# Windowed attention and two gated layers on one core: what the planner books for the attention's last steps

## The chip, the core and the metric

The kernel runs on one core of a Trainium2 chip. A core has five engines that run their own instruction streams in order: TensorE (PE; its weight loads are shown apart as PEld), VectorE (DVE), ScalarE (ACT), GpSimd (POOL) and SyncE (SP), which issues the DMA transfers here. The metric is the device time of one execution in microseconds (us); lower is better.

## What is computed

The reference, cut to what matters. Shapes: q, k, v are (4, 8, 576, 64); the token matrix between the parts is 2304 x 512.

```python
def _attn_ref(q, k, v):                      # causal, a window of 64 keys
    scores = scale * np.matmul(q, k.transpose(0, 1, 3, 2))
    mask = (rel >= 0) & (rel < 64)
    scores = np.where(mask, scores, -1e9)
    attn = np.exp(scores - np.max(scores, axis=-1, keepdims=True))
    attn = attn / (np.sum(attn, axis=-1, keepdims=True) + 1e-09)
    return np.matmul(attn, v)

x = attn_out.transpose(0, 2, 1, 3).reshape(2304, 512)
g = x @ w_gate                               # 512 x 1536
x = (g / (1 + np.exp(-g))) * (x @ w_val) @ w_out
h = (x @ w1) * (x @ w2) @ w3                 # 1024 wide
return h @ w_out2                            # 2304 x 512
```

The weights and the result keep fp32 accuracy; each fp32 operand is split into a high part and a remainder, and a product takes three passes (high x high, high x remainder, remainder x high).

## The kernel before

**Attention.** It runs in 24 steps, m = 0 to 23. In step m, PE computes the scores `S`, DVE takes their maximum (L420), ACT the exponential (L427), DVE the reciprocal of the sum (L433, L434), POOL multiplies it in (`pexp`, L437), PE transposes the result (`PT`, L446), DVE copies the transpose to SBUF (`ptt`, L452), PE multiplies by v (`PV`, L466), and ACT copies that into the token tiles `X` (L480, L483). The stages are staggered: `PT` of step m is made two steps later and `PV` three steps later, so after the loop an end is left over: one `PV`, and two times `PT`, `ptt`, `PV`. After the loop ACT also loads another function table (L563).

**Operands.** The first gated layer takes its tokens in three groups of 768 (tp = 0, 1, 2). A group is cut in four blocks by seven-product (Strassen-like) algebra; for each product p (in the order 1, 2, 5, 6, 7, 4, 3) and each half m of the 512 channels there is a tile `xo_pm`, made of up to three jobs: a difference of X blocks, in place (L208, DVE), a cast to the high part (L200, ACT), and the remainder (L204, DVE). In the names below the group is left out; the number at a name's end tells tiles of different groups apart. Differences for product 6 overwrite what product 5 reads, so they follow the remainder of 5.

**The gated layer.** `gated` yields one product at a time: six matmuls of 128x384 (L596) into a PSUM bank (`ala`, `gaa`, `bea` for the gate weights, `alb`, `gab`, `beb` for the value weights), then a copy by ACT (L603), additions by DVE (L607), SiLU by ACT (L617) and the gating product by DVE (L614). Units run in the order (gate, value) for group 0, 1, 2, with the products of two units interleaved; then come the next 256 columns of the weights, which first have to be narrowed from 64-bit words and split (L188, L190, L192, L194, L200, L204, L208).

**The planner.** The order of instructions on each engine is fixed when the program is built. Jobs (operand and weight preparation) lie in a queue with costs per engine. The code of the attention and of the products is written out at once, and the planner keeps a clock `plan.now`: `plan.charge` books written work on an engine, `plan.advance(us, but)` lets time pass and then emits every queued job that its books let start before the clock, on engines not in `but`. A job that is emitted early stands ahead of the attention's or the product's own instructions on its engine. `plan.slots` counts free SBUF tiles in the same way, and `hold` gives back those that the attention no longer needs. None of these numbers runs on the chip; they only set the order. Near the attention's end four functions use them: `during_attention` at the end of a step, `filling` inside a step, `drain(0..4)` after the loop (three of its calls take a product from the generator `gate`), and `operands(tp)`, which queues a group's operand jobs.

Of the kernel before, what the change touches and what calls it, by code (L numbers as in the profile page):

```python
# [32 lines left out]
def window_attention_moe_kernel(ctx: ExitStack, tc: tile.TileContext, q, k, v, w_gate, w_val, w_out, w1, w2, w3, w_out2, out):  # L33
# [121 lines left out]
    plan = Plan()  # L155
# [173 lines left out]
    def x_tile(tp, c):  # L329
        if (tp, c) not in X:  # L330
            X[tp, c] = slot([P, TP], F32, f"X{tp}_{c}")
        return X[tp, c]

    def attention(events, filling, drain):
        if True:
            ident, identr = own.tile([P, P], F32, name="ident"), own.tile([P, P], F32R, name="identr")
# [179 lines left out]
            for m in range(NM):  # L516
# [24 lines left out]
                if m == NM - 1:  # L541

                    evac_PT(m - 2)
                else:

                    filling(m)
# [7 lines left out]
                if m == NM - 1:  # L554
                    filling(m)
# [6 lines left out]
            evac_PV(NM - 3)  # L562
            nc.scalar.activation(out=masks[:, 0, :1], in_=masks[:, 1, :1], func=AF.Silu)  # L563
            drain(0)
            for x in range(2):
                emit_PT(NM - 2 + x)
                evac_PT(NM - 2 + x)
                drain(1 + 2 * x)
                emit_PV(NM - 2 + x)
                evac_PV(NM - 2 + x)  # L570
                drain(2 + 2 * x)
# [509 lines left out]
    def loads(n):  # L1081
        while at[0] < min(n, len(coming)):
            coming[at[0]].load()
            at[0] += 1

    def make_to(x, rank=None):

        while at[1] <= coming.index(x):
            plan.rank = rank if rank is not None else 1 if isinstance(coming[at[1]], Weights) else 2
            loads(at[1] + 1)  # L1090
            coming[at[1]].make()
            at[1] += 1
            loads(at[1] + 2)
            plan.rank = 0
# [72 lines left out]
    gate = gated(xop1, left1, order1, AF.Silu, h1d, events1)  # L1167


    HELD = {18: 24, 19: 22, 20: 18, 21: 16, 22: 12, 23: 7}  # L1170
# [3 lines left out]
    def hold(n):  # L1174
        plan.slots += held[0] - n
        held[0] = n

    def operands(tp):
        xop1[tp] = Operands([X[tp, c] for c in range(KC)], f"xo{tp}")

    def during_attention(m):
        if m in HELD:
            hold(HELD[m])
        if m in (1, 3):
            loads(1 + m // 2)
        if m == 3:
            make_to(left1[0, 1], 0)
        if m in (13, 20):
            operands(m // 20)
        plan.fill(("DVE",) if m not in HELD or m < 23 else ("DVE", "ACT"))  # L1190

    def filling(m):
        for e, cost in (("DVE", 2.75), ("ACT", 3.2), ("POOL", 2.6)):
            plan.charge(e, cost)
        if m == 23:
            plan.advance(3.1, ("DVE", "ACT", "POOL", "SP"))
        else:
            plan.advance(3.85, ("ACT", "POOL", "SP"))

    def drain(n):  # L1200
        hold(HELD_END[n])
        for e, cost in (("DVE", (0.4, 1.1, 0.0, 1.1, 0.0)), ("ACT", (3.0, 0.0, 0.6, 0.0, 0.6))):
            plan.charge(e, cost[n])
        if n == 4:
            operands(2)
        else:
            next(gate) if n in (0, 1, 3) else plan.advance(0.8)

    with tc.manual_schedule():
        plan.shut.add("POOL")  # L1210
        attention(during_attention, filling, drain)
        plan.ahead = 1.0
        for _ in gate:
            pass
        for _ in project(rows, wos, events_p):
            pass
        on(events2, len(order2) - 6, lambda: make_to(w3s[-1]))
        begin_e, run_e = final(rows2)

        def put_all():  # L1220
            for j in by:
                plan.need(j)
            begin_e()
        on(events2, len(order2) - 4, put_all)
        for _ in gated(xop2, left2, order2, AF.Copy, h2d, events2):
            pass
        run_e()
# [30 lines left out]
```

## Time and profile before

| | us |
|---|---|
| median of three runs | 851.5 (849.07 to 853.0) |
| the profiled execution, its own time | 851.86 |
| its span, first to last instruction | 850.1 |
| PE busy in the span | 826.2 (97%) |
| PEld busy | 794.4 (93%) |
| DVE busy | 644.5 (76%) |
| ACT busy | 451.6 (53%) |
| POOL busy | 61.4 (7%) |

Time outside the span is 1.8 us. A row of the time-ordered view gives start, duration, engine, line, operation, output and input tile, shape and, in square brackets, how long the engine sat idle before it and what released it. Neighbouring rows of one engine overlap slightly, because a row includes the pipeline's end: the distance from start to start is the pace.

### The profile page before, as it was taken

The page shows a single profiled execution, that of the slowest core. Times are in us where ns is not written, and L with a number is a line of the kernel's source. Part 1 is how long each engine was busy: PE and PEld are TensorE (multiplying, and loading weights), DVE is VectorE, ACT ScalarE, POOL GpSimd, SP SyncE. Part 2 cuts the span into 40 slices and gives each one's busy share as a digit, 9 for nine tenths or more (in the row PEclk, how much of TensorE's full clock was granted, in tenths as well). Part 3 has the DMA queues.
Part 4 walks back from the last instruction along what each step waited for, and adds up shares of the span by engine and source line. Part 5 has one row for each costly group of instructions (what it writes and reads, how often), then busy time and mean ns, then how long its engine had stood idle before and what let it go on. Part 6 is the DMA issues. An engine that isn't in the chain of part 4 may idle for free.

```text
span 850.1 us, 15759 instructions
## 1 busy us (share of the span) xinstructions
PE 826.2 (97%) x5870; PEld 794.4 (93%) x5870; DVE 644.5 (76%) x1364; ACT 451.6 (53%) x1188; POOL 61.4 (7%) x89
## 2 busy tenths in 40 slices
PE   7899979899999999999999999999999999999998
PEld 5788768899999999999999999999999998889998
DVE  4699877868688767876689585678788844788884
ACT  6799864564647464643454362444444423666452
POOL 3467700000000000000000000000000000000000
PEclk9899998999999999999999999999999999999999
DMA  9998200125265324679996861014456329623522
GB/s 184 230 178 204 80 1 38 38 96 213 88 222 186 123 114 161 223 281 380 367 291 192 242 216 50 1 74 145 147 179 176 121 74 354 220 71 128 175 75 75
DMA packets 147516, 136.29 MB, mean 160 GB/s; under 512 B 95088, under 2 KB 114288, under 8 KB 146416
## 3 DMA queue, kind: packets, MB, share of 16 engines
q1 hardware_dynamic: 147440, 135.29, 51.0%
q8 instruction: 46, 0.75, 0.4%
q14 instruction: 30, 0.25, 0.1%
HBM read 92.27 MB, written 42.99 MB: 159 GB/s over the span
## 4 chain that ended last, share of the span: by engine, by line
PE 85%; DMA 6%; DVE 4%; SPq 3%; ACT 1%; issue 1%; DVEq 0%; ACTq 0%
PE ala L596 15%; PE alb L596 14%; PE o L736 12%; PE beb L596 7%; PE bea L596 7%; PE al L960 6%; PE acc L894 5%; PE gab L596 4%; PE gaa L596 3%; PE be L960 3%; DMA wo<-wo 2%; PE PV L466 2%; PE PT L446 2%; PE S L413 2%; PE ga L960 2%; PE T L376 2%
## 5 line engine op out<-in xcount | busy, mean ns | idle before, releaser
L736 PE MATMUL o<-ph,wo 128*128 128x384 f32 x576 | 146.5, 334 | 0.7 <-DVE X L723 0.7
L736 PEld LDWEIGHTS o<-ph,wo 128*128 128x128 f32 x576 | 104.0, 188 | 1.0 <-DVE X L723 1.0
L736 PE MATMUL o<-pl,wo 128*128 128x384 f32 x288 | 96.3, 334 | 0.5 <-DVE pl L204 0.5
L603 ACT COPY ha<-ala 128x384 f32<-128x384 f32 x90 | 42.7, 477 | 58.8 <-PE ala L596 53.1
L607 DVE TENSOR_TENSOR ha<-ha,bea 128x384 f32<-128x384 f32 x60 | 33.2, 553 | 36.6 <-PE bea L596 20.1
L736 PEld LDWEIGHTS o<-pl,wo 128*128 128x128 f32 x288 | 54.1, 188 | 0.8 <-DVE pl L204 0.8
L427 ACT ACTIVATE pexp<-S,stat 128x128 f32<-128x128 f32 x144 | 53.8, 432 | 0.0
L617 ACT ACTIVATE ha<-ha 128x384 f32<-128x384 f32 x54 | 28.4, 525 | 37.4 <-DVE ha L607 37.4
L204 DVE TENSOR_TENSOR hf<-h,hf 128x384 fp32r<-128x384 f32 x84 | 43.5, 552 | 5.7 <-ACT hf L200 5.6
L200 ACT CAST ph<-pl 128x768 fp32r<-128x768 f32 x36 | 29.2, 837 | 34.8 <-DMA pl<-h 28.0
L200 ACT CAST hf<-h 128x384 fp32r<-128x384 f32 x84 | 39.3, 514 | 13.0 <-DVE h L208 11.4
L204 DVE TENSOR_TENSOR pl<-pl,ph 128x768 fp32r<-128x768 f32 x36 | 33.5, 952 | 13.9 <-ACT ph L200 13.4
L437 POOL TENSOR_TENSOR pexp<-pexp,stat 128x384 f32<-128x384 f32 x48 | 39.3, 840 | 41.7 <-DVE stat L434 38.1
L603 ACT COPY c12b<-alb 128x384 f32<-128x384 f32 x30 | 14.4, 480 | 49.8 <-PE alb L596 49.7
L427 ACT ACTIVATION_READ_ACCUMULATOR pexp<-S,stat 128x1 f32 x144 | 38.3, 270 | 0.0
L607 DVE TENSOR_TENSOR c22b<-c22b,beb 128x384 f32<-128x384 f32 x30 | 16.6, 554 | 27.5 <-ACT c22b L603 27.5
L420 DVE TENSOR_REDUCE stat<-S 128x3 f32<-128x384 f32 x48 | 24.4, 550 | 7.2 <-PE S L413 7.0
L596 PE MATMUL ala<-xo,w_g_1h 128*128 128x384 f32 x120 | 27.1, 338 | 2.1 <-ACT w_g_1h L200 2.1
L204 DVE TENSOR_TENSOR xo<-X,xo 128x384 fp32r<-128x384 f32 x42 | 24.1, 598 | 4.8 <-ACT xo L200 4.8
L930 ACT COPY o<-al 128x256 f32<-128x256 f32 x36 | 13.4, 373 | 27.0 <-PE al L960 26.0
L452 DVE COPY ptt<-PT 128x384 f32<-128x384 f32 x48 | 23.8, 536 | 4.6 <-PE PT L446 4.6
L603 ACT COPY c11b<-alb 128x384 f32<-128x384 f32 x30 | 14.3, 477 | 23.0 <-PE alb L596 23.0
(526 smaller groups left out, 2501.9 us busy)
## 6 DMA issues: line engine op xcount, KB each, us to landing
h<-ha SPq DMA_DIRECT2D x60, 384.0 KB, 3.1
pl<-h SPq DMA_DIRECT2D x36, 384.0 KB, 6.5
h<-h SPq DMA_DIRECT2D x24, 384.0 KB, 4.5
st_w<-in_moe_w_dram SPq DMA_DIRECT2D x8, 1024.0 KB, 5.7
st_g<-in_moe_w_gate_dram SPq DMA_DIRECT2D x6, 1024.0 KB, 6.2
st_v<-in_moe_w_val_dram SPq DMA_DIRECT2D x6, 1024.0 KB, 5.4
st_wo<-in_moe_w_out_dram SPq DMA_DIRECT2D x6, 1024.0 KB, 5.2
wo<-by_wo SPq DMA_DIRECT2D x12, 512.0 KB, 3.8
```

The lines of the kernel that those rows point to most:

```text
L200: (eng.copy if eng is nc.scalar else eng.tensor_copy)(out=hi(), in_=src())
L204: return plan.job(lambda eng: eng.tensor_tensor(out=lo(), in0=src(), in1=hi().bitcast(F32), op=ALU.subtract), after, slots=slots, DVE=dve( ...
L420: nc.vector.tensor_reduce(out=st[:, 0, x, :], in_=sc[2 * m + x], op=ALU.max, axis=AX.X, negate=True)
L427: nc.scalar.activation(out=pe[:, jj, :], in_=so[:, jj, :], func=AF.Exp, bias=st[:, 0, x, jj:jj + 1], accum_out=st[:, 1, x, jj:jj + 1])
L437: nc.gpsimd.tensor_tensor(out=pe, in0=pe, in1=st[:, 3, x, :].unsqueeze(2).to_broadcast([P, SUB, P]), op=ALU.mult)
L596: nc.tensor.matmul(acc, lhsT=self.wt.ops[p, x][:, m, :], rhs=self.xs.ops[p, m][:, y, :], start=start and n == 0, stop=n == 5, skip_group_c ...
L603: nc.scalar.copy(out=out, in_=src)
L607: nc.vector.tensor_tensor(out=out, in0=x, in1=y, op=ALU.add)
L617: nc.scalar.activation(out=h, in_=src, func=func)
L736: nc.tensor.matmul(acc[m, x], lhsT=wos.tiles[i // 6][:, i % 6, :], rhs=rows[2 * tp + x].words(f, b), start=f == n == 0, stop=f == NF - 1 a ...
L894: nc.tensor.matmul(acc, lhsT=w3T[i][c // 3][:, x, (c % 3) * P:(c % 3) * P + P], rhs=zt[c, y], start=c == k == 0, stop=c == NI - 1 and k == 2)
L960: nc.tensor.matmul(acc, lhsT=self.xs.ops[p, m][:, x, t * P:t * P + P], rhs=right.ops[p, m, y], start=start and n == 0, stop=n == 3 * R - 1 ...
```

## The change

Five edits to numbers and order in the planner's calls; no instruction's work is changed. (1) At the end of step 22 ACT is left out of the filling, as DVE is in every step; before, ACT was left out in step 23 alone. (2) Inside step 22 the clock passes 3.1 us with no engine to be filled, as in step 23, where before it passed 3.85 us and DVE was filled. (3) In `drain`, call 0 books 1.4 us on DVE instead of 0.4, and 1.6 us on ACT instead of 3.0. (4) Each call of `drain` lets 0.65 to 0.9 us pass, which fills all engines but POOL, ahead of a product, where before only call 2 let 0.8 us pass. (5) The products of calls 0, 1 and 3 come after that.

```diff
-        plan.fill(("DVE",) if m not in HELD or m < 23 else ("DVE", "ACT"))
+        plan.fill(("DVE",) if m < 22 else ("DVE", "ACT"))
...
-        if m == 23:
+
+        if m >= 22:
             plan.advance(3.1, ("DVE", "ACT", "POOL", "SP"))
         else:
             plan.advance(3.85, ("ACT", "POOL", "SP"))

     def drain(n):
         hold(HELD_END[n])
-        for e, cost in (("DVE", (0.4, 1.1, 0.0, 1.1, 0.0)), ("ACT", (3.0, 0.0, 0.6, 0.0, 0.6))):
+        for e, cost in (("DVE", (1.4, 1.1, 0.0, 1.1, 0.0)), ("ACT", (1.6, 0.0, 0.6, 0.0, 0.6))):
             plan.charge(e, cost[n])
+
+        plan.advance((0.9, 0.7, 0.85, 0.65, 0.85)[n])
+        if n in (0, 1, 3):
+            next(gate)
         if n == 4:
             operands(2)
-        else:
-            next(gate) if n in (0, 1, 3) else plan.advance(0.8)
```

The order of work on PE, on POOL and of the DMA issues on SP stays as it was but for the names of weight tiles. DVE and ACT change from step 22 to the first weights of the next 256 columns. On DVE, from the maximum of step 22 to the first copies of `ptt`, this stood before (`stat` are the attention's sums, `xo_50_1977` and `xo_30_1894` operands of group 0):

```order
L420 TENSOR_REDUCE stat_2023<-S_1981 128x3
L204 TENSOR_TENSOR xo_50_1977<-X_0_447,xo_50_1977 128x384
L204 TENSOR_TENSOR xo_30_1894<-X_2_698,xo_30_1894 128x384
L433 TENSOR_SCALAR stat_1956<-stat_1956 128x6
L434 RECIPROCAL stat_1956<-stat_1956 128x6
L452 COPY ptt_2059<-PT_2011 128x384
L452 COPY ptt_2059<-PT_2015 128x384
```

Now the two remainders are gone from there. The first stands after the loop, ahead of the next to last `ptt`; the second comes some twenty instructions later still. On DVE, the end after the loop was, before:

```order
L434 RECIPROCAL stat_2087<-stat_2087 128x6
L204 TENSOR_TENSOR xo_51_2041<-X_1_528,xo_51_2041 128x384
L208 TENSOR_TENSOR X_0_447<-X_2_698,X_0_447 128x384
L452 COPY ptt_2145<-PT_2137 128x384
L452 COPY ptt_2145<-PT_2141 128x384
L607 TENSOR_TENSOR ha_0_0_2125<-ha_0_0_2125,gaa_0_2148 128x384
L452 COPY ptt_2180<-PT_2172 128x384
L452 COPY ptt_2180<-PT_2176 128x384
L204 TENSOR_TENSOR xo_60_2204<-X_0_447,xo_60_2204 128x384
```

and is now:

```order
L434 RECIPROCAL stat_2083<-stat_2083 128x6
L204 TENSOR_TENSOR xo_50_1977<-X_0_447,xo_50_1977 128x384
L452 COPY ptt_2140<-PT_2132 128x384
L452 COPY ptt_2140<-PT_2136 128x384
L607 TENSOR_TENSOR ha_0_0_2121<-ha_0_0_2121,gaa_0_2145 128x384
L204 TENSOR_TENSOR xo_51_2143<-X_1_528,xo_51_2143 128x384
L208 TENSOR_TENSOR X_0_447<-X_2_698,X_0_447 128x384
L452 COPY ptt_2181<-PT_2173 128x384
L452 COPY ptt_2181<-PT_2177 128x384
L208 TENSOR_TENSOR X_1_528<-X_3_776,X_1_528 128x384
L204 TENSOR_TENSOR xo_60_2193<-X_0_447,xo_60_2193 128x384
```

The difference for product 6 (`X_0_447`) has gone from ahead of the next to last `ptt` to ahead of the last. On ACT the same stretch, from the first SiLU to the copy of product 6, was before (X_2_1801 and X_3_1884 are the tokens that the last two `PV` fill):

```order
L617 ACTIVATE ha_0_0_2125<-ha_0_0_2125 128x384
L483 COPY X_2_1801<-PV_2157 128x192
L483 COPY X_3_1884<-PV_2157 128x192
L480 COPY X_3_1884<-PV_2190 128x384
L200 CAST xo_60_2204<-X_0_447 128x384
L200 CAST xo_61_2208<-X_1_528 128x384
L603 COPY ha_0_0_2125<-ala_0_2127 128x384
```

and is now:

```order
L617 ACTIVATE ha_0_0_2121<-ha_0_0_2121 128x384
L200 CAST xo_31_2155<-X_3_776 128x384
L483 COPY X_2_1801<-PV_2157 128x192
L483 COPY X_3_1884<-PV_2157 128x192
L200 CAST xo_10_2184<-X_0_952 128x384
L200 CAST xo_60_2193<-X_0_447 128x384
L200 CAST xo_11_2195<-X_1_1120 128x384
L480 COPY X_3_1884<-PV_2198 128x384
L200 CAST xo_61_2213<-X_1_528 128x384
L603 COPY ha_0_0_2121<-ala_0_2123 128x384
```

Four casts, among them that of product 6, now stand ahead of the last copy from PSUM. The third place is DVE at the seam from group 0 to group 1 (`xo_50_2316` and `xo_50_2319` are operands of group 1, `c22b_0` and `ha_0` belong to group 0, `ha_1` to group 1). Before:

```order
L607 TENSOR_TENSOR c22b_0_2338<-c22b_0_2338,beb_0_2270 128x384
L614 TENSOR_TENSOR ha_0_1_2126<-ha_0_1_2126,c22b_0_2338 128x384
L607 TENSOR_TENSOR ha_1_0_2318<-ha_1_0_2318,gaa_1_2344 128x384
L204 TENSOR_TENSOR xo_50_2316<-X_0_952,xo_50_2316 128x384
L204 TENSOR_TENSOR xo_51_2330<-X_1_1120,xo_51_2330 128x384
L208 TENSOR_TENSOR X_0_952<-X_2_1209,X_0_952 128x384
```

and now:

```order
L204 TENSOR_TENSOR xo_50_2319<-X_0_952,xo_50_2319 128x384
L204 TENSOR_TENSOR xo_30_2272<-X_2_1209,xo_30_2272 128x384
L607 TENSOR_TENSOR c22b_0_2342<-c22b_0_2342,beb_0_2276 128x384
L614 TENSOR_TENSOR ha_0_1_2122<-ha_0_1_2122,c22b_0_2342 128x384
L607 TENSOR_TENSOR ha_1_0_2322<-ha_1_0_2322,gaa_1_2348 128x384
L204 TENSOR_TENSOR xo_51_2346<-X_1_1120,xo_51_2346 128x384
L208 TENSOR_TENSOR X_0_952<-X_2_1209,X_0_952 128x384
```

The remainder of `xo_50` has passed ahead of three of the products' own instructions; that of `xo_51` stays behind them. At the seam from group 1 to group 2 the order is now the same as this one; before, both remainders stood ahead there.

## Rows read from the trace of the kernel before

**Rows 1.** The page: busy time of each engine, with its share of the span.

```profile
PE 826.2 (97%) x5870; PEld 794.4 (93%) x5870; DVE 644.5 (76%) x1364; ACT 451.6 (53%) x1188; POOL 61.4 (7%) x89
```

**Rows 2.** Busy time by stretch: PE, PEld, DVE, ACT, POOL, clock, DMA share, GB/s.

```profile
109.00:123.50 14.50, 12.95 (x67) 11.51 (x67) 11.77 (x24) 10.44 (x26) 0.00 (x0) 1.00 0.01 2
123.50:127.80 4.30, 1.43 (x7) 0.82 (x5) 3.79 (x8) 3.04 (x9) 0.00 (x0) 0.93 0.00 0
127.80:130.70 2.90, 2.46 (x7) 2.06 (x8) 2.90 (x7) 0.40 (x1) 0.00 (x0) 0.50 0.00 0
...
160.20:164.50 4.30, 4.28 (x16) 4.12 (x17) 2.71 (x7) 2.24 (x6) 0.00 (x0) 0.63 0.00 0
...
168.00:200.00 32.00, 32.00 (x186) 32.00 (x185) 23.13 (x49) 18.26 (x40) 0.00 (x0) 1.00 0.44 157
200.00:850.00 650.00, 645.14 (x3885) 635.29 (x3884) 486.59 (x998) 310.88 (x672) 0.00 (x0) 1.00 0.51 171
```

**Rows 3.** In order of time, steps 22 and 23: DVE and PE.

```profile
95.26 1.88 DVE L204 TENSOR_TENSOR xo<-X,xo 128x384 fp32r<-128x384 f32 x2
...
98.03 0.94 PE L466 MATMUL PV<-ptt,v 128*64 128x64 f32 x24 [0.97 <-DVE ptt L452]
```

**Rows 4.** In order of time, after the loop: DVE and PE.

```profile
101.98 1.02 DVE L204 TENSOR_TENSOR xo<-X,xo 128x384 fp32r<-128x384 f32 x1
...
102.93 1.18 DVE L208 TENSOR_TENSOR X<-X,X 128x384 f32<-128x384 f32 x1
...
104.04 1.01 DVE L452 COPY ptt<-PT 128x384 f32<-128x384 f32 x2
104.73 0.94 PE L466 MATMUL PV<-ptt,v 128*64 128x64 f32 x24 [0.48 <-DVE ptt L452]
```

**Rows 5.** In order of time, the last PV to product 7 of group 0.

```profile
107.45 0.92 PE L466 MATMUL PV<-ptt,v 128*64 128x64 f32 x24
108.41 0.48 ACT L480 COPY X<-PV 128x384 f32<-128x384 f32 x1 [1.92 <-PE PV L466]
...
109.36 0.44 PE L596 MATMUL ala<-xo,w_g_5l 128*128 128x384 f32 x1 [0.99 <-ACT xo L200]
...
112.00 1.21 PE L596 MATMUL alb<-xo,w_v_1h 128*128 128x384 f32 x6
...
115.13 0.51 PE L596 MATMUL gab<-xo,w_v_1h 128*128 128x384 f32 x2
...
118.92 1.96 DVE L204 TENSOR_TENSOR xo<-X,xo 128x384 fp32r<-128x384 f32 x4
```

**Rows 6.** In order of time, the seam from group 0 to group 1.

```profile
123.45 0.34 PE L596 MATMUL bea<-xo,w_g_2l 128*128 128x384 f32 x1
...
125.04 0.54 DVE L607 TENSOR_TENSOR ha<-ha,gaa 128x384 f32<-128x384 f32 x1
...
126.11 0.44 PE L596 MATMUL bea<-xo,w_g_2l 128*128 128x384 f32 x1 [2.32 <-DVE xo L204]
...
130.69 2.12 PE L596 MATMUL alb<-xo,w_v_4h 128*128 128x384 f32 x6
...
132.61 1.87 PE L596 MATMUL beb<-xo,w_v_3h 128*128 128x384 f32 x6
...
136.40 0.51 PE L596 MATMUL gab<-xo,w_v_1h 128*128 128x384 f32 x2
```

**Rows 7.** In order of time, PE at the seam from group 1 to group 2.

```profile
144.72 0.51 PE L596 MATMUL bea<-xo,w_g_2l 128*128 128x384 f32 x2
...
148.64 1.20 PE L596 MATMUL alb<-xo,w_v_4h 128*128 128x384 f32 x6
```

**Rows 8.** In order of time, PE at the first weights of the next columns.

```profile
160.22 1.56 PE L596 MATMUL ala<-xo,w_g_1h 128*128 128x384 f32 x6 [2.05 <-ACT w_g_1h L200]
...
166.27 0.44 PE L596 MATMUL bea<-xo,w_g_6h 128*128 128x384 f32 x1 [0.64 <-DVE w_g_6h L204]
...
168.11 1.20 PE L596 MATMUL alb<-xo,w_v_4h 128*128 128x384 f32 x6
```

## The prediction

> **What bounds the kernel now.** I read the page first: PE is busy for 826.2 us, 97% of the span [rows 1]. So the time can only fall where PE waits, or runs at the lower of its two clock levels. Next I read busy time by stretch. From 168 us to 200 us PE is busy for 32.00 of 32.00 us, and from there to 850 us for 645.14 of 650 [rows 2]; the change reorders nothing there but a few weight casts. What PE loses, it loses between the attention's last steps and 168 us, and once it is full behind that, each microsecond that it arrives earlier should reach the end. So the question is when PE reaches the product that starts at 168.11 [rows 8].
>
> The time-ordered view of 95 to 170 us, engine by engine, then gives the losses. One product without a wait takes 1.04 us: the eight from 115.13 to 123.45 take 8.32 [rows 5, 6]. Against that PE loses 0.97 at the PV of 98.03 [rows 3], 0.48 at that of 104.73 [rows 4], 2.6 from the last PV's end (109.36 - 0.99 = 108.37) to 112.00, where one product would take 1.04, and 1.05 from 112.00 to 115.13, which is two products [rows 5]. From 123.45 two products take 7.24 us, not 2.08, with one wait of 2.32, and the next three run partly at clock 0.50, the 1.2 GHz level, where a product takes 1.92 (130.69 to 132.61) [rows 2, 6]. From 144.72 two products take 3.92 [rows 7]. Then come 2.05 us of waiting for the next weights and a stretch at clock 0.63 [rows 2, 8]. In nearly all of these the releaser is DVE or ACT, which PE overtakes: operands are made just too late, in an order that the planner chose.
>
> **The change, step by step.** No DMA issue and no work of POOL is moved, so no queue is passed; I follow DVE and ACT in the new order, with durations of the rows, and write where PE then stands. All clock times below are in the profiled execution of before.
>
> Step 22 loses two remainders on DVE that took 1.88 us (95.26) [rows 3]. The reciprocal and the `ptt` copies behind them start that much earlier, and are done before PE's scores end at 98.03 - 0.97 = 97.06. The PV starts at 97.06: **-0.97**. The cast taken off ACT there has no one waiting.
>
> After the loop one remainder and one difference stood ahead of the next to last `ptt`; they took 1.02 and 1.18 [rows 4], twice the pace of the same instructions later (four in 1.96 [rows 5]); POOL is multiplying beside them. One remainder is left there, and the difference follows. The copy that began at 104.04 comes 0.97 + 1.11 (start to start) earlier, which is more than its wait, and PE's own products set the next PV: 104.73 - 0.97 - 0.48, and some 0.25 of queue between, gives 103.0. The last PV then moves from 107.45 to about 105.6: **-0.9** more. The remainder is taken at its slow price; at the later one the `ptt` would be ready 0.5 sooner and PE would not notice.
>
> Product 6 needs its casts. Before, ACT idled 1.92 us until it could copy the last PV (108.41), and cast only then; PE waited 0.99 for it and some more for the remainders [rows 5]. Now the cast for half 0 stands ahead of that copy, in that idle time, so four casts of about the copy's 0.48 us cost nothing; without that cover they would delay the copy by 1.9 us. The last PV ends at 106.5; the first half's remainder is done at 106.7; the copy runs to 106.95 and the second cast to 107.35; its remainder (0.49 each, 1.96 for four [rows 5]) to 107.9. So the next product starts at 108.3 and not at 112.00: -3.7, of which **-1.85** is new. Product 7 then waits 0.35 for a remainder, not 1.05: `gab` at 110.7, not 115.13, **-0.7**, -4.4 in sum. The eight products behind find their operands, so the seam begins at 119.0, not 123.45.
>
> At the seam, before, PE waited 2.32 for a remainder that stood behind the addition of 125.04 [rows 6]. Now the first remainder stands ahead. But DVE works through group 0's additions and nine operand instructions (0.49 each) from 113.3 to 117.2, ACT's SiLU and cast behind them take it to 118.2, and with two remainders and two additions (0.54 each) the addition of this seam comes at 120.5, not 125.04, and the second remainder, still behind it, is done at 121.45: PE waits 0.3 and 1.5, and in product 6 another 0.45 and 0.75 while DVE makes three differences and two remainders. Product 6 ends at 124.15; before it ended at 130.69: -6.55, **-2.1** new. The four products behind it took 5.71 (130.69 to 136.40), partly at the low level, instead of 4.16: **-1.55** if the clock now stays up. Sum -8.0.
>
> At the next seam the new order is worse, since the second remainder now stands behind an addition: two products take about 4.55, not 3.92 [rows 7]: **+0.65**.
>
> At the next weights the chain is the same, but a remainder (0.49) is gone from ahead of it and both halves are scaled by ACT ahead of a SiLU: I get a wait of 1.65 instead of 2.05: **-0.4**. From 160.22 to 168.11 five products took 7.89, partly at the low level and with a wait of 0.64 [rows 2, 8]. In the new order the remainder that PE waited for stands earlier, but the next one stands behind three instructions of the products, and costs 0.9. At the full level this makes 6.3: **-1.6**.
>
> The sum with the clock up throughout is -0.97 - 0.9 - 1.85 - 0.7 - 2.1 - 1.55 + 0.65 - 0.4 - 1.6 = **-9.4 us**. The two remainders that DVE now makes later (0.98) cost nothing more, since DVE has 14.50 - 11.77 = 2.7 us idle between 109 and 123.5 alone [rows 2]; if that cover were gone they would come back in full.
>
> **The clock is the unknown cost.** Here it fell to 0.50 after PE had been idle 2.32 us in one piece, and to 0.63 after 2.05 in one piece; it was 1.00 over 109 to 123.5, where each wait is 1 us or less [rows 2, 5]. In the new schedule the seam has 3.0 us of waits in four pieces, the longest 1.5; the second seam 2.4 in three pieces, the longest 1.1; the weights 1.65 in one. None of these is among the rows. From below a fall costs 0. From above: the first low stretch lasted from about 127.8 to at least 134.3, where the product of 132.61 (1.87 long) makes room; of these 6.5 us each 1.92 holds 0.88 of loss, so 3.0 us. I take 2.5 for one fall, at the first seam, the heaviest. Likeliest then: -9.4 + 2.5 = -6.9.
>
> The Trainium skill (TensorE: Matmul & The Clock Gate, "What's actually happening") says that the low level is the default, that recent activity releases it, and that the activity is watched on a clock of its own, not one that begins with the kernel. By that rule the same waits may drop the clock in one build and not in another, and the sum lies anywhere from -9.4 to the case of three falls. The trace agrees in so far as both falls came within a few microseconds of a long wait; whether the phase counts, two falls cannot show.
>
> **The rivals.**
> *The clock stays up.* -9.4: 842.1. For it: the longest single wait is shorter than both that preceded a fall. Against: the pieces at the first seam together are as long.
> *Two falls.* -9.4 + 5.0 = -4.4: 847.1. For it: the second seam's 2.4 us, and its wait is made by the change.
> *DVE is the bound, and only the attention's end is gained.* Then the gated layer spends the lead waiting at the first seam: between -0.97 - 0.9 = -1.9 and -3.7, so 847.8 to 849.6. For it: DVE is busy for 3.79 of 4.30 us in the seam and 2.90 of 2.90 behind it [rows 2]. Against: it idled 2.7 us ahead of that, and the remainder that PE waited for has moved up.
> *The change does nothing*: the next wait eats the gain at the PV at once; within 1 us of 851.5. Against: the waits of 0.48 and 0.99 behind it are released by work that moves forward with it or ahead of it [rows 4, 5].
> *Slower: the clock falls at the first seam and does not rise.* The new order strews short waits over the gated layer (0.3 to 1.5 us each, by the schedule above), and if they keep the clock at 1.2 GHz, each microsecond there loses 0.46 (0.88 of 1.92). From 20.5 us of low clock on, all of the 9.4 is gone; from the first seam to the next weights, some 30 us, it costs 14: -9.4 + 14 = +4.6, 856. For it: the clock did fall at this place. Against: it rose again within 7 us as soon as products followed without a wait, and a slow PE waits less.
>
> **How the numbers follow.** The profiled execution took 851.86 us, 0.36 above the median of the runs, 851.5; I take the gain from the median: 851.5 - 6.9 = **844.6**. Chances: one fall 0.36, none 0.24, two 0.20, the attention's end alone 0.12, nothing 0.04, slower 0.04. The range runs from 840.5 (no fall, and 1.6 for runs that differ, as the three of before do by up to 2.4 from their median) to 849.0 (the attention's end alone): 8 in 10. About 0.5%, 4.3 us, is what a measurement of this kernel can tell from no change. Faster by more is 847.2 or less, which takes one fall, none, and two thirds of two: 0.74. The rest of two, the attention's end and nothing make up 0.22, slower is 0.04.
>
> **What would show it.** The PV of step 23 without a wait; the last PV ending 1.9 us earlier, near 106.5; `alb` of group 0 near 108.3; the first seam at 119.0 with several waits under 1.6 us and none of 2.3; the second seam's product 6 slower than 3.92 for the two; the product now at 168.11 near 161. The clock column by stretch decides between none, one and two falls. I am wrong if a cast or remainder that was moved ahead delays the last PV beyond 107.4, if PE waits anew behind 168 us, or if the operands of group 1 come later than 119.

## The result, and the profile after

The changed kernel takes 843.34 us (median of six runs, 840.73 to 845.66). Before, with three runs more than the table above has, it is 849.63 us (849.07 to 853.0). The ratio is 0.9915, with a 95% interval of 0.9889 to 0.9940: 0.85% faster. (The ratio is nearer to that of the means, 843.06 to 850.32, than to that of the medians.) The profiled execution of after took 841.41 us with a span of 839.7.

The page's first part, after, against [rows 1]:

```profile
PE 819.7 (98%) x5870; PEld 788.6 (94%) x5870; DVE 642.9 (77%) x1364; ACT 451.0 (54%) x1188; POOL 60.9 (7%) x89
```

PE does the same 5870 matmuls in 6.5 us less busy time: a row counts longer at the low clock, and 5.4 of the 6.5 lie in the three stretches in which before's clock fell (the start, the first seam and what follows it, the products behind the weights). The windows of [rows 2], after (PE, PEld, DVE, ACT, POOL, clock, DMA share, GB/s):

```profile
109.00:123.50 14.50, 12.18 (x64) 10.88 (x64) 12.96 (x28) 11.19 (x27) 0.00 (x0) 1.00 0.01 2
123.50:127.80 4.30, 4.30 (x27) 4.30 (x26) 4.25 (x10) 2.19 (x5) 0.00 (x0) 1.00 0.00 0
127.80:130.70 2.90, 2.90 (x18) 2.90 (x17) 2.30 (x6) 1.02 (x3) 0.00 (x0) 1.00 0.69 271
160.20:164.50 4.30, 4.30 (x26) 4.30 (x26) 3.59 (x8) 1.70 (x4) 0.00 (x0) 1.00 0.65 222
168.00:200.00 32.00, 32.00 (x186) 32.00 (x186) 24.64 (x54) 17.39 (x40) 0.00 (x0) 1.00 0.36 128
```

The clock is 1.00 in every stretch, where before had 0.50 and 0.63; in this execution it did not fall here at all. The time-ordered view of PE, after (start, duration, what, idle time before it), with the rows that answer to [rows 3] to [rows 8]:

```profile
92.86 0.94 PE L466 MATMUL PV<-ptt,v 128*64 128x64 f32 x24
...
95.76 0.92 PE L466 MATMUL PV<-ptt,v 128*64 128x64 f32 x24
...
97.81 1.03 PE L466 MATMUL PV<-ptt,v 128*64 128x64 f32 x24 [0.24 <-DVE ptt L452]
...
101.89 0.92 PE L466 MATMUL PV<-ptt,v 128*64 128x64 f32 x24
...
104.59 0.92 PE L466 MATMUL PV<-ptt,v 128*64 128x64 f32 x24
...
106.50 1.03 PE L596 MATMUL ala<-xo,w_g_5l 128*128 128x384 f32 x2 [0.27 <-ACT xo L200]
...
107.55 1.21 PE L596 MATMUL alb<-xo,w_v_1h 128*128 128x384 f32 x6
...
110.27 0.52 PE L596 MATMUL gab<-xo,w_v_1h 128*128 128x384 f32 x2
...
118.61 0.51 PE L596 MATMUL bea<-xo,w_g_2l 128*128 128x384 f32 x2
...
121.11 0.44 PE L596 MATMUL bea<-xo,w_g_2l 128*128 128x384 f32 x1 [1.26 <-DVE xo L204]
...
123.96 1.20 PE L596 MATMUL alb<-xo,w_v_4h 128*128 128x384 f32 x6
...
136.44 0.51 PE L596 MATMUL bea<-xo,w_g_2l 128*128 128x384 f32 x2
...
141.22 1.20 PE L596 MATMUL alb<-xo,w_v_4h 128*128 128x384 f32 x6
...
152.46 1.44 PE L596 MATMUL ala<-xo,w_g_1h 128*128 128x384 f32 x6 [1.71 <-ACT w_g_1h L200]
...
158.98 1.20 PE L596 MATMUL alb<-xo,w_v_4h 128*128 128x384 f32 x6
```

The PV of step 23 (95.76) has lost its wait, product 6 waits 0.27 for its second cast, and no wait at the first seam is longer than 1.26. The last row is the product that stood at 168.11 before. But part of this lead is older than the edits. Before, the PV made in step 22, where DVE and ACT still have the old order, starts at

```profile
94.09 0.94 PE L466 MATMUL PV<-ptt,v 128*64 128x64 f32 x24
```

and after at 92.86. In the twelve further profiles it starts at 92.64 to 93.74, one of them with the old code throughout (92.73); before's profiled execution came late out of its start. Its clock had fallen there too, a third fall beside the two of the rows ahead of the prediction; before, same columns as above:

```profile
24.00:28.00 4.00, 2.80 (x31) 2.49 (x32) 1.49 (x5) 0.91 (x3) 2.27 (x4) 0.60 1.29 217
28.00:32.00 4.00, 4.00 (x38) 3.25 (x38) 1.48 (x3) 2.56 (x14) 0.50 (x1) 0.54 0.76 183
```

Whether that made it late, no run shows. So I count by stretches, each from the start of one landmark to the start of the next:

| stretch | before | predicted change | after | change |
|---|---|---|---|---|
| start to the PV made in step 22 | 94.09 | 0 | 92.86 | -1.23 |
| to the last PV | 13.36 | -1.87 | 11.73 | -1.63 |
| to `gab` of group 0 | 7.68 | -2.55 | 5.68 | -2.00 |
| to the first seam | 8.32 | 0 | 8.34 | +0.02 |
| first seam, two products | 7.24 | -2.1 | 5.35 | -1.89 |
| to the second seam | 14.03 | -1.55 | 12.48 | -1.55 |
| second seam, two products | 3.92 | +0.65 | 4.78 | +0.86 |
| to the next weights | 11.58 | -0.4 | 11.24 | -0.34 |
| five products | 7.89 | -1.6 | 6.52 | -1.37 |
| to the end of the span | 681.99 | 0 | 680.72 | -1.27 |

The stretches where the change acts give -7.90; the first, which the edits do not reach, and the last, in which they change the order on DVE and ACT for some 20 us while PE does not wait, give -2.50; together the 10.4 us between the two spans.

The runs that were only timed report a mean clock, and after's times follow it: 841.41 and 840.73 at 1.000, 843.27 at 0.998, 843.89 and 843.40 at 0.996, 845.66 at 0.994. Before's eleven runs of the first set below lie at 0.989 to 0.994.

### The profile page after: what moved, and what is told of

It reads as the page before. It is cut to its first block, busy times and chain, and to the rows that moved or that the text cites. A ratio compares the mean times of both kernels' runs of the same rounds, so it can differ in the third digit from the quotient of the medians.

```text
span 839.7 us, 15766 instructions
## 1 busy us (share of the span) xinstructions
PE 819.7 (98%) x5870; PEld 788.6 (94%) x5870; DVE 642.9 (77%) x1364; ACT 451.0 (54%) x1188; POOL 60.9 (7%) x89
## 4 chain that ended last, share of the span: by engine, by line
PE 83%; DMA 8%; SPq 3%; DVE 3%; ACT 2%; issue 1%; DVEq 0%; ACTq 0%
PE ala L596 14%; PE alb L596 14%; PE o L736 12%; PE bea L596 7%; PE beb L596 7%; PE al L960 6%; PE acc L894 5%; PE gab L596 3%; PE gaa L596 3%; PE be L960 3%; DMA wo<-wo 2%; PE PV L466 2%; PE PT L446 2%; SPq L350 2%; DMA zd<-by_z 2%; PE S L413 2%
## 5 line engine op out<-in xcount | busy, mean ns | idle before, releaser
L596 PE MATMUL ala<-xo,w_g_6l 128*128 128x384 f32 x90 | 29.6, 338 | 0.7 <-DVE w_g_6l L204 0.5
```

The lines of the kernel that those rows point to most:

```text
L596: nc.tensor.matmul(acc, lhsT=self.wt.ops[p, x][:, m, :], rhs=self.xs.ops[p, m][:, y, :], start=start and n == 0, stop=n == 5, skip_group_c ...
```

## The experiments

Each kernel was timed in five rounds beside the kernel before on the same chip; the ratio is to that. The code is cut: `...` marks what is left out. "Fillers" are matmuls into a bank whose content is thrown away, so nothing of the result changes with them.

**Edits 1 and 2 alone** (steps 22 and 23; `drain` as before).

```diff
-        plan.fill(("DVE",) if m not in HELD or m < 23 else ("DVE", "ACT"))
+        plan.fill(("DVE",) if m < 22 else ("DVE", "ACT"))
...
-        if m == 23:
+        if m >= 22:
```

> Only the edits of steps 22 and 23 (no filling there); the calls of drain stay as before. My theory, that most of the gain comes from the order after the loop: the PV of step 23 starts without its wait of 0.97 us, but both remainders taken out of step 22 now stand ahead of the next to last ptt, and the casts of product 6 stay behind the last copy of X; the first seam keeps its wait of more than 2 us and the clock falls there as before. Expected -0.5 to -1.5 us against before. Rival, that the two remainders in step 22 were the cost: -4 us or more.

Measured 846.03 us, ratio 0.9956 (0.9940 to 0.9971): -3.6 us, far more than expected and near the rival's -4. The rows show why: with the two remainders gone from step 22 the planner, still with the old books, also sets the first cast of product 6 ahead of the last X copy, so `alb` follows the last PV after 2.96 us, as in after, and not after 4.55. What I had put down to the drain's edits comes with these two as well.

**Edits 3 to 5 alone** (the steps as before, `drain` as in the diff above):

```diff
-        for e, cost in (("DVE", (0.4, 1.1, 0.0, 1.1, 0.0)), ("ACT", (3.0, 0.0, 0.6, 0.0, 0.6))):
+        for e, cost in (("DVE", (1.4, 1.1, 0.0, 1.1, 0.0)), ("ACT", (1.6, 0.0, 0.6, 0.0, 0.6))):
...
+        plan.advance((0.9, 0.7, 0.85, 0.65, 0.85)[n])
+        if n in (0, 1, 3):
+            next(gate)
...
```

> Only the edits of drain (bookings, time that passes, order of the products); steps 22 and 23 are filled as before. My theory: the PV of step 23 waits 0.97 us as before, the casts of product 6 stand ahead of the last copy of X, and from there on the gated layer runs as in the changed kernel: -5 to -7 us against before. Rival (steps 22 and 23 are the source): no more than -2 us.

Measured 845.57 us, ratio 0.9945 (0.9925 to 0.9965): -4.1, between the two theories. From the PV made in step 22 to the end of the first seam's two products before takes 36.60 us, edits 1 and 2 34.63, edits 3 to 5 33.33, after 31.10: the parts, -2.0 and -3.3, nearly add up to the whole, -5.5. The shorter seam needs both: two products take 6.53 and 6.54 with either part, 5.35 with both; for edits 1 and 2, 0.79 of that difference is a fall of the clock (below); the clock of edits 3 to 5 is as low there (0.79 over 123 to 131 us in both), but has not been priced.

**Fillers in the waits of after.**

```diff
+    def extra(self, acc, w, n):
+        for _ in range(n):
+            nc.tensor.matmul(acc, lhsT=w, rhs=self.xs.ops[1, 0][:, 0, :], start=True, stop=True)
...
+    if seam:
+        self.extra(self.be, self.wt.ops[2, 0][:, 0, :], (9, 6)[self.tp - 1])
     self.mm(self.be, 5, True)
...
```

> The changed kernel with matmuls that are thrown away, in a bank that is cleared or free, ahead of the waits at both seams (9 and 4, 6 and 4) and of the first weights of the next columns (9): the order on DVE and ACT is that of the changed kernel, and PE's idle time there shrinks from 1 to 2 us a place to a few tenths. My theory, that the changed kernel's runs differ because the clock falls in some of them behind these waits: granted clock 1.000 in every run, runs within about 1 us of each other, at the changed kernel's fastest level, -8.5 to -9.5 us against before's median. Rival (the runs differ for another reason, such as the first loads): the same spread of 5 us, and a median like that of the changed kernel, -6 to -7 us, or slower by what the extra matmuls add.

Measured 841.20 us (840.67 to 841.66), ratio 0.9902 (0.9888 to 0.9915). The mean clock is 0.998 in all four runs, and they spread over 1.0 us, where after's six spread over 4.9; the intervals of the two ratios overlap. In the profiled execution the 0.002 that are left lie elsewhere, at the kernel's start (windows of 20 to 36 us, same columns):

```profile
24.00:28.00 4.00, 4.00 (x50) 3.40 (x54) 1.90 (x5) 3.21 (x16) 2.78 (x4) 0.70 1.34 209
28.00:32.00 4.00, 4.00 (x68) 3.24 (x64) 1.99 (x4) 2.08 (x10) 0.00 (x0) 0.88 0.85 261
```

That fall costs nothing: PE only waits less for its transfers afterwards (over 32 to 36 us it is busy for 3.37, where after, without that fall, has 2.17), and the PV made in step 22 starts at 92.78.

**Operands pulled ahead of the products' own additions** (DVE and ACT; at both seams and at the weights).

```diff
+    if first and self.x == 0 and self.tp:
+        rests = [self.xs.jobs[6, m] for m in range(2)]
+        for j in [r.after[0].after[0] for r in rests] + rests:
+            pull(j)
...
+    if first and self.x and self.tp < NTP - 1:
+        pull(xop[self.tp + 1].jobs[5, 0])
+        pull(xop[self.tp + 1].jobs[5, 1])
...
```

`pull` writes a queued job out at once; in product 6 of group 2's value unit it does so for the first weights too.

> The changed kernel with three places put in another order: the second remainder of product 5 and the differences and remainders of product 6 go ahead of the additions at both seams, and the first weights of the next columns are narrowed and split ahead of the gating additions there. My theory, that what is left at these places is order and not a shortage of DVE: the seams lose under 1 us each instead of 3.4 and 2.7, the weights 0.5 instead of 1.9, so -4 to -6 us more than the changed kernel, and no fall of the clock. Rival (DVE is the bound between 109 and 150 us): the waits move behind the seams, and the gain is under 2 us.

Measured 844.72 us, ratio 0.9941 (0.9927 to 0.9955): 4 to 6 us more than after were expected, and nothing came; the median is 1.4 us above after's, though the intervals overlap. The waits went behind the seams. PE, with what it waits for (lines are shifted by seven):

```profile
151.31 0.44 PE L603 MATMUL ala<-xo,w_g_2l 128*128 128x384 f32 x1 [1.14 <-DVE xo L211]
154.54 1.44 PE L603 MATMUL ala<-xo,w_g_1h 128*128 128x384 f32 x6 [1.55 <-ACT w_g_1h L207]
159.62 0.44 PE L603 MATMUL bea<-xo,w_g_7h 128*128 128x384 f32 x1 [1.20 <-DVE w_g_7h L211]
```

The two products of the first seam take 4.63 us instead of 5.35, but the stretch to the next weights 12.78 instead of 11.24. So the rival holds: here DVE and ACT are the bound, and pulling one operand forward puts another back.

**Fillers in the kernel before.** How much of the change is the clock?

```diff
+    self.extra(self.be, self.wt.ops[2, 0][:, 0, :], (14, 2)[self.tp - 1])
     self.mm(self.be, 5, True)
...
```

> The kernel before, with matmuls that are thrown away (14 and 4 ahead of products 5 and 6 at the first seam, 2 and 4 at the second, 11 ahead of the first weights of the next columns); the order on DVE and ACT is that of before. Theory (the change gains on two accounts, shorter waits and fewer clock falls): before's profile lost 0.24 of 8 us, 0.06 of 24 us and 0.11 of 15 us to the low clock, 5.0 us together; with TensorE kept busy most of that comes back, so 845 us (844 to 846.5), every run at a clock of 0.997 or more, and the 3 to 5 us that are left to the kernel after with the same fillers (841.2) are what the order itself gives. Rival A, the falls cost nothing: 849 to 850. Rival B, the falls were nearly all of it: 841 to 842.5.

Measured 848.60 us (eleven runs), ratio 0.9983 (0.9975 to 0.9992). My theory was wrong: the mean clock of these runs is that of after (0.995 to 1.000, on average 0.997), and only 1.2 us come back. Windows and PE, this kernel:

```profile
109.00:123.00 14.00, 13.46 (x68) 12.74 (x67) 10.75 (x23) 10.59 (x26) 0.00 (x0) 0.88 0.01 2
123.00:131.00 8.00, 7.37 (x41) 6.68 (x40) 7.56 (x16) 4.84 (x13) 0.00 (x0) 1.00 0.00 0
```

```profile
122.59 2.59 PE L629 MATMUL bea<-xo,w_g_1h 128*128 128x384 f32 x14
...
128.06 0.44 PE L596 MATMUL ala<-xo,w_g_5l 128*128 128x384 f32 x1 [0.63 <-DVE xo L204]
```

The first seam, fillers and all, takes 6.45 us instead of 7.24 and its clock stays up, but in this execution the clock fell earlier instead, behind product 6's waits of 0.15 to 0.99. With fillers on both sides the change is worth 0.9902 / 0.9983 = 0.9919, without them 0.9915. Since this kernel kept a fall in spite of its fillers, the runs at full clock say more: its three with a mean clock of 1.000 took 846.47, 847.18 and 849.27 us, after's two 840.73 and 841.41. With the clock up in both, the gain is about as large: over the runs it is not the clock's.

**Fillers with edits 1 and 2.**

```diff
+    self.extra(self.be, self.wt.ops[2, 0][:, 0, :], (12, 2)[self.tp - 1])
     self.mm(self.be, 5, True)
...
```

> Edits 1 and 2 alone, with thrown-away matmuls (12 and 2 at the first seam, 2 and 7 at the second, 11 ahead of the weights). Edits 1 and 2 alone measured 846.03 and their profile lost 0.21 of 8 us to the low clock. Theory (much of their 3.6 us was a fall that no longer came, not order): with the falls kept out of both, 844.3 us (843.5 to 845.2), 0.3 to 1.5 us under the kernel before with its fillers. Rival (their order gives the 3.6 us by itself): 3 us or more under the kernel before with its fillers.

Measured 845.38 us, ratio 0.9942 (0.9930 to 0.9954): 3.2 us under before with its fillers. The rival holds: edits 1 and 2 gain their 3 us by order.

**One wait made longer**, without and with fillers.

```diff
     self.add(self.c11, self.c11, ga)
+    if func != AF.Copy and (self.fp, self.x, self.tp) == (0, 0, 1):
+        for _ in range(2):
+            nc.vector.tensor_copy(out=ga, in_=ga)
```

> The kernel after, with two copies of a bank onto itself on DVE (some 0.5 us each) ahead of the last remainder of product 5 at the first seam: its wait of 1.26 us grows to about 2.3 us, as long as the one before the change. Theory (a wait of that length drops the clock): 1.0 us for the wait and 1.5 to 2.5 us for a fall in every run, so 846.5 us (845.3 to 847.5), a granted clock under 0.9 in the 8 us behind the seam. Rival (only the wait counts): 844.3 us (843.8 to 844.8) and the clock behind the seam at 1.00.

> The same two copies in the kernel with fillers, with 15 instead of 9 thrown-away matmuls ahead of product 5 at the first seam. Theory (the wait alone, its fall kept out): 841.2 + 1.0 = 842.2 us (841.7 to 842.8), the clock at 1.00 behind the seam, so that the difference to the kernel with the copies and no fillers prices a fall at 3 to 5 us together with what the fillers give elsewhere. Rival (a fall comes anyway, or the fillers get in the way): 844 us or more.

Measured 844.97 us (843.19 to 848.72), ratio 0.9944 (0.9928 to 0.9961), without, and 843.24 (842.58 to 845.10), ratio 0.9923 (0.9912 to 0.9935), with fillers. PE from the first of the two products at the seam to the product behind them, and the window there, without fillers:

```profile
118.39 0.51 PE L596 MATMUL bea<-xo,w_g_2l 128*128 128x384 f32 x2
...
121.94 0.44 PE L596 MATMUL bea<-xo,w_g_2l 128*128 128x384 f32 x1 [2.33 <-DVE xo L204]
...
125.58 1.93 PE L596 MATMUL alb<-xo,w_v_4h 128*128 128x384 f32 x6
```

```profile
123.00:131.00 8.00, 7.58 (x33) 7.33 (x34) 6.18 (x13) 3.28 (x8) 0.00 (x0) 0.79 0.05 18
```

and PE from the first filler to the same product, with fillers:

```profile
118.91 2.76 PE L629 MATMUL bea<-xo,w_g_1h 128*128 128x384 f32 x15
...
125.32 1.22 PE L596 MATMUL alb<-xo,w_v_4h 128*128 128x384 f32 x6
```

As foretold, a wait of 2.33 us brought a fall (all six runs have a mean clock of 0.993 to 0.996), and with fillers it did not come (clock 1.00 in the same window). But 844.97 lies below the theory's 845.3 to 847.5, nearer to the rival's 844.8, and the difference of the two kernels is 1.7 us, not 3 to 5. Two products at the seam take 7.19 without fillers and 6.41 with them; the stretch behind 13.24 and 12.50: 1.52 us for the fall. The two other pairs agree at the seam: before 7.24 and 6.45, edits 1 and 2 6.53 and 5.74, each time 0.78 or 0.79; behind it 1.52 and 0.43. So one fall cost 1.2 to 2.3 us. The wait itself cost what its length says: 6.41 against the 5.35 of after with fillers is 1.06. The kernel with fillers still missed its 842.2 (841.7 to 842.8): in its profiled execution, the slowest of the five, waits of 0.8 and 0.7 us stand far behind this place; for the others the cause is not shown.

**The change without edit 3, and without edits 4 and 5**, both with the fillers of 841.20.

```diff
-  (("DVE", (1.4, 1.1, 0.0, 1.1, 0.0)), ("ACT", (1.6, 0.0, 0.6, 0.0, 0.6)))
+  (("DVE", (0.4, 1.1, 0.0, 1.1, 0.0)), ("ACT", (3.0, 0.0, 0.6, 0.0, 0.6)))
```

> The change without edit 3 (the old books 0.4 us on DVE and 3.0 us on ACT in the first call), with the fillers of the kernel that measured 841.2 us. Theory (the smaller ACT book is what puts product 6's casts early and opens the first seam sooner, as the prediction's steps have it): 843.5 to 845.5 us, near the 845.4 of edits 1 and 2 alone with fillers, and the two products of the first seam at about 6.5 us, fillers included, where the whole change has 5.35. Rival (passing time in each call does it, whatever is booked): 841 to 842 us and 5.3 us at the seam.

```diff
-        plan.advance((0.9, 0.7, 0.85, 0.65, 0.85)[n])
-        if n in (0, 1, 3):
-            next(gate)
         if n == 4:
             operands(2)
+        else:
+            next(gate) if n in (0, 1, 3) else plan.advance(0.8)
```

> The change without edits 4 and 5 (time passes only in the third call, after which no product comes), with the same fillers: edits 1, 2 and 3. On DVE the first two remainders of product 5 and the first difference now stand behind the two copies of ptt instead of ahead of them. Theory (the books carry the drain's gain): 841.5 to 842.7 us, at most 1.5 us over the 841.2 of the whole change with fillers. Rival (passing time carries it): 844 to 845.5 us.

Measured 843.96 us, ratio 0.9926 (0.9915 to 0.9938), without the books, and 844.11, ratio 0.9933 (0.9919 to 0.9947), without the passing time. The second was expected at 842.7 at most: both are needed, and they lose about the same against 0.9902 (0.9888 to 0.9915; the first interval just touches it). The first time is as expected, but not for the reason given: the two products of the first seam take 5.15 us and not 6.5, and `alb` follows the last PV after 2.38 us, sooner than the 2.96 of after. So product 6's casts come early without the smaller ACT book too; without edit 3 the time is lost ahead of the last PV (14.23 us from the PV of step 22, where the whole change with fillers has 11.73) and 1.0 us more behind the second seam. DVE and PE at the drain's first `ptt` show why. Without edit 3, DVE:

```profile
99.60 2.14 DVE L204 TENSOR_TENSOR xo<-X,xo 128x384 fp32r<-128x384 f32 x2
101.66 1.18 DVE L208 TENSOR_TENSOR X<-X,X 128x384 f32<-128x384 f32 x1
102.76 1.01 DVE L452 COPY ptt<-PT 128x384 f32<-128x384 f32 x2
```

and PE behind it:

```profile
103.45 0.94 PE L466 MATMUL PV<-ptt,v 128*64 128x64 f32 x24 [1.58 <-DVE ptt L452]
```

Without edits 4 and 5, DVE:

```profile
100.87 1.06 DVE L452 COPY ptt<-PT 128x384 f32<-128x384 f32 x2 [0.68 <-PE PT L446]
...
104.69 1.01 DVE L204 TENSOR_TENSOR xo<-X,xo 128x384 fp32r<-128x384 f32 x2
```

and PE:

```profile
105.29 0.44 PE L596 MATMUL bea<-xo,w_g_2l 128*128 128x384 f32 x1 [1.08 <-DVE xo L204]
```

and the whole change, DVE:

```profile
99.69 1.03 DVE L204 TENSOR_TENSOR xo<-X,xo 128x384 fp32r<-128x384 f32 x1
100.65 1.01 DVE L452 COPY ptt<-PT 128x384 f32<-128x384 f32 x2
```

Three operand instructions ahead of the `ptt` make the PV wait 1.58 us, two (edits 1 and 2 alone) 0.47. With none DVE idles 0.68 us ahead of the `ptt`, and product 5 then waits 1.08 for a remainder. One, of 1.03 us, nearly fits into that idle time, and the PV of 101.89 does not wait. Time that passes with the old books puts three there, the new books without it none.

**TensorE's order at the seams**: products 4 and 3 of the group before put into the waits of 5 and 6, and the first product of the next columns one later.

```diff
-  when = [(7 * n + AT[p], n, p) ...
+  late = {(2, 5): 5.5, (2, 6): 6.5, (4, 5): 5.5, (4, 6): 6.5, (6, 1): 1.5} if func != AF.Copy else {}
+  when = [(7 * n + late.get((n, p), AT[p]), n, p) ...
```

> The kernel after, no fillers, with TensorE's own order changed: at both seams the value products 4 and 3 of the group before stand ahead of and between products 5 and 6, and the first product of the next columns stands one product later. Theory (at the seams TensorE waits for DVE and ACT, so ready products put into the wait come free): products 5, 6, 4, 3 took 7.4 us at the first seam and 6.9 at the second, 4.2 of that work; here 5.5 to 6.5 at each, and the wait for the first weights of the next columns goes from 1.7 to 0.7 us; together 2.5 to 4 us under after, so 839.5 to 841 us, waits of no more than 1.3 us and a clock of 0.996 or more in every run. Rival (the gating products that DVE owes for 4 and 3 now stand ahead of its remainders, so the wait moves along): 842.5 to 844 us.

Measured 842.31 us, ratio 0.9906 (0.9893 to 0.9919), not to be told from after's 0.9915 and short of the 839.5 to 841 expected. From the PV made in step 22, the value product 1 of group 1 starts after 32.57 us instead of 33.18, that of group 2 after 49.39 instead of 50.44: 0.6 and then 1.05 us won in all, not 2. The weights lost it again. PE:

```profile
142.15 0.44 PE L596 MATMUL ala<-xo,w_g_5l 128*128 128x384 f32 x1 [1.49 <-DVE xo L204]
...
152.66 0.62 PE L596 MATMUL ala<-xo,w_g_1h 128*128 128x384 f32 x2 [0.81 <-ACT w_g_1h L200]
154.55 0.44 PE L596 MATMUL ala<-xo,w_g_1l 128*128 128x384 f32 x1 [1.27 <-DVE w_g_1l L204]
```

The wait of 1.71 became two, of 0.81 and 1.27, and the clock fell to 0.90 over 155 to 172 us.

**The seam part of it with fillers**, the weights left as they were.

```diff
+  late = {(2, 5): 5.5, (2, 6): 6.5, (4, 5): 5.5, (4, 6): 6.5} if func != AF.Copy else {}
...
+    self.extra(self.ga, self.wt.ops[2, 0][:, 0, :], (3, 7)[self.tp - 1])
     self.mm(self.al, 6)
...
```

> The seam part of the run before (products 4 and 3 of the group before into the waits of products 5 and 6), without the later product at the weights, which lost there what the seams had won (two waits of 0.81 and 1.27 us and a clock of 0.90 over 17 us), and with fillers in the waits that are left: 2 and 3 at the first seam, 7 at the second, 9 ahead of the weights. Theory: the seams win 0.6 and 0.45 us as in that run, on the 841.2 us of the kernel with fillers, so 840.2 us (839.5 to 841), clock 0.998 or more in every run. Rival (the later differences of the groups delay the weights' preparation on DVE): 841.5 us or more.

Measured 840.71 us, ratio 0.9895 (0.9878 to 0.9911): the fastest kernel here, 1.05% under before, as expected; against 0.9902 without the new product order the intervals overlap.

## Why the prediction was right, step by step

The forecast was 844.6, the measurement 843.34; 6.9 us were predicted and 6.3 came by the medians. That the two lie so near is in part luck. The forecast was counted from 851.5; from the 849.63 that three more runs gave, it would have been 842.7. And the sum without a fall was 1.5 us too large, while the first and the last stretch, which it put at nothing, gave 2.5. The steps, by the table above:

- **The end of the attention** (-0.97 and -0.9): -1.63 measured, of which 1.04 stands ahead of the PV of step 23, which starts without a wait, and 0.59 behind it. The slow remainder, reckoned at 1.02, took 1.03.
- **Products 6 and 7** (-1.85 and -0.7): -2.00. Product 6's first half finds its cast; the second waits 0.27. The step stands, but edits 1 and 2 and edits 3 to 5 each bring most of it by themselves.
- **First seam** (-2.1): -1.89. The waits 0.3, 1.5, 0.45 and 0.75 came as 0.3, 1.26, 0.40 and 0.42, and the rest, 5.35 - 2.38 = 2.97, is 0.9 more than the 2.08 of two products without a wait. 0.79 of it is the clock, by the pair with fillers. One reckoning ahead of it does not add up: nine operand instructions of 0.49 are 4.4 us and do not fit between 113.3 and 117.2; that the seam's addition came at 120.03, near the 120.5 foretold, is luck.
- **Clock up behind the seam** (-1.55): -1.55 in the profiled execution, which is one without a fall. Four of after's five other runs have a lower mean clock and are 1.9 to 4.3 us longer. That fits the one fall that I took as likeliest, but a mean clock does not tell where the clock fell, and a fall at the start cost nothing (above).
- **Second seam** (+0.65): +0.86. **Weights** (-0.4): -0.34. **Five products behind them** (-1.6): -1.37, of which 0.71 is the clock (7.89 against 7.18 with fillers in before).

In this pair of profiles, then, some 3.0 of the 7.9 us are the clock (0.79, 1.52 and 0.71), since the one execution had falls and the other none; 4.9 are the order.

Every sign was right and the sum too large: -9.4 against -7.9, with no step off by more than 0.6. The term that was mis-sized is the fall, 2.5 against 1.2 to 2.3. What I drew from the Trainium skill (TensorE: Matmul & The Clock Gate, "What's actually happening"), that the same waits may drop the clock in one build and not in another, agrees with the runs: a wait of 2.05 us for the next weights was followed by clock 0.63 before [rows 2, 8] and by 1.00 over 155 to 170 us with edits 1 and 2 and with edits 3 to 5.

The rival that only the attention's end is gained is out, since `gab` and the first seam kept the lead. So is a clock that stays low: no profile shows one over all of 123 to 160 us. The rival of a clock that stays up is the profiled execution, 841.41 against its 842.1, and the kernel with fillers, 841.20.

What stays open: the 1.27 us behind 168 us. That tail takes 680.2 to 681.3 us in ten profiles and 682.0 to 683.0 in the two of before's order (without and with fillers) and in two others. It is made of single waits of 0.2 to 0.8 us in changing places, and no experiment was aimed at it. Between before and after PE keeps its distance from 168 us of before up to 410; 1.0 us comes at 410 to 437 and 0.3 at 716, where the traces show the same order on every engine in both. Between the two with fillers it is 5.4 us from the PV of step 22 to the product behind the weights and 1.4 behind that: a fifth of the gain is put down to no step.

## What to carry to other kernels

Where PE overtakes the engines that make its operands, as here, the number of preparing instructions ahead of a hand-over matters: count them against the idle time in front of it, and add no more than fit (here one, with three costing 1.58 us and none 1.08). Before a gain is put down to the clock, put fillers into the old kernel as well as into the new one; here that showed that the clock does not explain the difference of the kernels. And pull work ahead only where the engine that does it has idle time, or the wait moves along.

## What the runs showed of the hardware

- A fall of the clock at the same place cost 1.2, 1.5 and 2.3 us in three pairs of profiles: each time 0.78 or 0.79 in the two products of the seam, and 0.43 to 1.52 behind it.
- The length of one wait does not decide alone. Waits of 2.08 to 2.33 us at the first seam were followed by a fall in all four kernels that had them; one of 2.05 at the weights was followed by a fall in one of three; two of 0.81 and 1.27, ending 1.9 us apart, also brought one; and in before with fillers one came behind waits of 0.99, 0.15 and 0.39, where the same waits in before (0.99, 0.16 and 0.39) brought none.
- Some 32 thrown-away matmuls (about 0.17 us each) in waits went with a spread of 1.0 us (four runs) instead of after's 4.9 (six) and a median 2 us lower; 35 in before took 1.2 off, and its runs spread over 3.4 us, where those without spread over 2.1.
- The clock does not explain all of a kernel's spread: three runs of the last kernel above, all at a mean clock of 1.000, took 840.46, 840.55 and 842.61 us.
